# Two heads in one DMA transpose, the hash in row and column tiles, and TensorE in an order fixed by hand

## The chip, the cores and the metric

The kernel runs on one core of a Trainium2 chip. The metric is device time in microseconds (us), from the program's start to its end on that core. A run has a state, "fast" or "slow" (slow: more than 1.5% above the fastest run of the same kernel). The clock is the share of its full speed that TensorE was granted, 0.50 being half. In the profiler's lines PE is TensorE, PEld its weight loads, DVE VectorE, ACT ScalarE, POOL GpSimd and SP SyncE; a q behind the name is the engine's queue, which here issues transfers.

## The reference, cut to what matters

There are 4 batches, 8 heads, 768 tokens per head and 64 features. Each query and each key gets six bits from the signs of a projection, and a query attends only to keys whose six bits equal its own. The attention's output goes through a gated feed-forward part with 3072 tokens, width 512 and hidden width 1536.

```python
q_bits = (np.einsum('bhsd,dk->bhsk', q, proj) > 0).astype(np.int64)
k_bits = (np.einsum('bhsd,dk->bhsk', k, proj) > 0).astype(np.int64)
...
scores = np.where(q_bucket[..., None] == k_bucket[:, :, None, :],
                  scale * np.matmul(q, k.transpose(0, 1, 3, 2)), -1e9)
attn = softmax(scores)                      # cut: exp, sum, divide
x = (attn @ v) as (3072, 512)
out = x + sigmoid(x @ w_res) * ((gelu(x @ w_gate) * (x @ w_val)) @ w_out)
```

## The kernel before

The mask is part of the scores' matmul. Behind the 64 features of a token stand 7 more rows: six hash bits of +-0.5, and a constant. The query features are scaled down by C and the exponential scales up again, so a pair of tokens that differs in a bit gets a very negative score. The scores therefore contract over 71 rows.

Work goes by pairs of heads (16 pairs, two pairs to a group). `prep` makes a group's operands: cast, hash, bits, transpose. It is a Python generator, advanced one piece per step of the attention.

```python
nat = [const.tile([P, HT, P], BF16) ...]         # HT = 12 blocks: 2 heads x 6
def prep(ps, first=False):
    hs = mm_ps.tile([P, HT, 32], FP32, tag="mm", name="hs")   # one PSUM bank
    for i, x in enumerate(jobs):                 # jobs: q and k of each pair
        cast(x, ...)                             # nat[:, :, 0:64] = bf16(raw)
    for h in range(2):
        ... # VectorE: tt = 32x32 block transposes of raw
        for dh in range(2):
            for j, tt in enumerate(t32):
                nc.tensor.matmul(hs[32 * j:32 * j + 32, h * T:(h + 1) * T, :],
                                 projw[:, dh, :], tt[:, :, dh, :], ...,
                                 tile_position=(0, 32 * j))    # column tiles only
        yield
    nc.vector.transpose(ht[:n], hs[:n])
    for j, x in enumerate(jobs):
        for a in range(4):                       # bits into nat[:, :, 64:70]
            nc.vector.tensor_scalar(nat_of(x)[32 * a:32 * a + 32, :, D:D + NBITS], ...)
        nc.sync.dma_start_transpose(out=ag, in_=nat_of(x))     # 12 blocks of 128x128
        aug[x] = ag
        yield
```

One step of the attention is a double bank of scores, one exponential over 128x1024, and the value matmuls of the step before. Each batch has 36 steps. The feed-forward part of batch b-1 is done during the attention of batch b: `gate_val` in one block, then `project` in pieces between the steps. The projection's two accumulators (`rps`, `fps`) and the hash share one pool of two PSUM banks, `mm_ps`.

```python
sc_ps = tile_pool("sc_ps", bufs=2, space=PSUM)   # scores: two double banks
av_ps = tile_pool("av_ps", bufs=2, space=PSUM)   # attention accumulators
mm_ps = tile_pool("mm_ps", bufs=2, space=PSUM)   # projection and hash
def scores(p, c):
    sp = sc_ps.tile([P, 1024], FP32, tag="sp", name="sp")
    ... # ks[0:71, block] x qs[0:71, up to 512 columns]
    nc.scalar.activation(e, sp, AF.Exp, scale=float(ALPHA))
    flush()                                      # the values of the step before
```

The softmax here doesn't subtract the row's maximum and nothing guards it: scores larger than these inputs give would overflow.

Of the kernel before, what the change touches and what calls it, by code (L numbers as in the profile page):

```python
# [9 lines left out]
FP32 = mybir.dt.float32  # L10
BF16 = mybir.dt.bfloat16
AF = mybir.ActivationFunctionType
ALU = mybir.AluOpType
# [4 lines left out]
def kernel(  # L18
# [11 lines left out]
):  # L30
    nc = tc.nc
    B, H, S, D = q.shape
    NBITS = proj.shape[1]
# [9 lines left out]
    NROW = NBITS + 1  # L43
    KA = D + NROW
    assert D == 64 and S == 768 and 4 * NBITS <= 32 and HP == KM

# [9 lines left out]


    projw = const.tile([P, 2, 32], FP32, name="projw")
    nc.vector.memset(projw, 0.0)
    for a in range(4):  # L60
        nc.scalar.dma_start(projw[32 * a:32 * a + 32, :, NBITS * a:NBITS * (a + 1)],
                            proj.rearrange("(h r) n -> r h n", r=32))
# [5 lines left out]

    NN = 4
    nat = []  # L70
    for i in range(NN):
        nat.append(const.tile([P, HT, P], BF16, name=f"nat{i}"))
        eng = nc.vector if i < 2 else nc.gpsimd
        eng.memset(nat[i][:, :, D:P], 0.0)
        eng.memset(nat[i][:, :, D + NBITS:KA], 1.0 if i % 2 == 0 else -NBITS / 4.0)

# [25 lines left out]
    ld_pool = ctx.enter_context(tc.tile_pool(name="ld", bufs=3))  # L102
    ldv_pool = ctx.enter_context(tc.tile_pool(name="ldv", bufs=2))
    aug_pool = ctx.enter_context(tc.tile_pool(name="aug", bufs=4))
    t32_pool = ctx.enter_context(tc.tile_pool(name="t32", bufs=5))
# [4 lines left out]
    av_ps = ctx.enter_context(tc.tile_pool(name="av_ps", bufs=2, space=PSUM))  # L110
    mm_ps = ctx.enter_context(tc.tile_pool(name="mm_ps", bufs=2, space=PSUM))

    raw, rawv, aug, vaug = {}, {}, {}, {}
# [14 lines left out]

    def nat_of(x):
        return nat[(2 * x[0] + x[1]) % NN]  # L130

    def cast(x, eng):
        scale = (1.0 / C) if x[1] == 0 else 1.0
        dst = nat_of(x)[:, :, 0:D]
        if eng is nc.scalar:
            nc.scalar.activation(dst, raw[x], AF.Copy, scale=scale)
        elif x[1] == 0:
            eng.tensor_scalar(dst, raw[x], scale, 1.0, op0=ALU.mult, op1=ALU.mult)  # L138
        else:
            eng.tensor_copy(dst, raw[x])  # L140

# [14 lines left out]
    def prep(ps, first=False):  # L156

        jobs = [(p, side) for p in ps for side in range(2)]
        n = 32 * len(jobs)
        hs = mm_ps.tile([P, HT, 32], FP32, tag="mm", name="hs")  # L160
        for i, x in enumerate(jobs):
            cast(x, nc.scalar if first and i == 0 else nc.gpsimd)
        yield
        for h in range(2):
            t32 = []
            for x in jobs:
                tt = t32_pool.tile([P, T, 2, 32], FP32, tag="t32", name="t32")
                nc.vector.transpose(tt.rearrange("p c h n -> p (c h n)"),  # L168
                                    raw[x][:, h * T:(h + 1) * T].rearrange("p c d -> p (c d)"))
                t32.append(tt)  # L170
                if len(t32) % 2 == 0:
                    yield
            for dh in range(2):
                for j, tt in enumerate(t32):
                    nc.tensor.matmul(hs[32 * j:32 * j + 32, h * T:(h + 1) * T, :],  # L175
                                     projw[:, dh, :], tt[:, :, dh, :],
                                     start=(dh == 0), stop=(dh == 1),
                                     tile_position=(0, 32 * j))
            yield
        ht = sm_pool.tile([P, HT, 32], FP32, tag="ht", name="ht")  # L180
        nc.vector.transpose(ht[:n].rearrange("p c n -> p (c n)"),
                            hs[:n].rearrange("p c n -> p (c n)"))
        for j, x in enumerate(jobs):
            del raw[x]
            for a in range(4):
                nc.vector.tensor_scalar(  # L186
                    nat_of(x)[32 * a:32 * a + 32, :, D:D + NBITS],
                    ht[32 * j:32 * j + 32, :, NBITS * a:NBITS * (a + 1)], 0.0, 0.5,
                    op0=ALU.is_gt, op1=ALU.subtract)
            ag = aug_pool.tile([P, HT, P], BF16, tag=f"aug{x[1]}", name=f"aug{x[1]}")  # L190
            nc.sync.dma_start_transpose(out=ag, in_=nat_of(x).rearrange("p c n -> p (c n)"))
            aug[x] = ag
            yield
        for p in ps:
            values_of(p)
            yield


    banks = []
    for hi in range(2):  # L200
        for i in range(T // 2):
            banks += [(hi, [(2 * i, 0, 4)]), (hi, [(2 * i + 1, 0, 4)]),
                      (hi, [(2 * i, 4, 2), (2 * i + 1, 4, 2)])]
    NCH = len(banks) // 2
    av = {}
# [15 lines left out]
    def values(p, c, e):  # L221
        va, vsum = vaug[p]
        for i in range(2):
            hi, parts = banks[2 * c + i]
            if (p, hi) not in av:
                o = av_ps.tile([P, T, D + 1], FP32, tag="av", name="av")
# [4 lines left out]
                    start=True, stop=False, skip_group_check=True)  # L231
            off = i * 512
            for (jt, qt0, nq) in parts:
                for qt in range(qt0, qt0 + nq):
# [3 lines left out]
                    off += P  # L238
            if (2 * c + i + 1) % NCH == 0:
                finish(p, hi)  # L240
# [7 lines left out]
    def scores(p, c):  # L248
        qs, ks = aug[p, 0], aug[p, 1]
        sp = sc_ps.tile([P, 1024], FP32, tag="sp", name="sp")  # L250
        for i in range(2):
            hi, parts = banks[2 * c + i]
            off = i * 512
            for (jt, qt0, nq) in parts:
                nc.tensor.matmul(sp[:, off:off + nq * P], ks[0:KA, hi * T + jt, :],  # L255
                                 qs[0:KA, hi * T + qt0:hi * T + qt0 + nq, :],
                                 start=True, stop=True)
                off += nq * P
# [28 lines left out]
    def project(b):  # L287

        hh = hidden.pop(b)
        for t in range(T):  # L290
# [4 lines left out]
            th = g_pool.tile([P, DMODEL], FP32, tag="th", name="th")  # L295
            nc.scalar.activation(th, rps, AF.Tanh, scale=0.5)  # L296
            yield
            fps = mm_ps.tile([P, DMODEL], FP32, tag="mm", name="fps")
            for m in range(KF):
                nc.tensor.matmul(fps, hh[:, m, bass.ts(t, P)], wo[:, m, :],  # L300
                                 start=(m == 0), stop=(m == KF - 1))
                if m % 3 == 2 and m < KF - 1:
# [5 lines left out]
                                           op0=ALU.mult, op1=ALU.add)  # L308
            nc.sync.dma_start(out_t[b, t], o)
            yield  # L310

# [17 lines left out]
    HELD = 6  # L329
    mlp = []  # L330

    def mlp_piece():
        while mlp:
            g = mlp[0]
            try:
                next(g[0])
                g[1] += 1
                return
            except StopIteration:
                mlp.pop(0)  # L340

    done = object()
    for g in range(NG):
# [61 lines left out]
```

## Time and profile before

| Before | Value |
|---|---|
| median of 2 runs | 407.11 us (406.05 to 408.16) |
| profiled run | span 404.7 us, mean clock 0.92 |
| part one: start to the first feed-forward matmul | 98.2 us |
| the three stretches that hold a feed-forward block beside attention | 84.3, 85.9, 78.1 us (sum 248.4 before rounding) |
| tail: the last feed-forward block | 58.2 us |

I call the three stretches "batches" below. They run from one block's first feed-forward matmul to the next block's first. Here they are as windows; the columns are length, busy time and instructions of PE, PEld, DVE, ACT and POOL, then clock, DMA share (1.00 means that all 16 DMA engines are busy) and GB/s.

```profile
0.00:98.18 98.18, 73.72 (x572) 35.36 (x575) 44.83 (x124) 42.20 (x42) 47.22 (x88) 0.68 1.11 225
98.18:182.50 84.32, 81.59 (x715) 47.20 (x725) 34.60 (x68) 51.14 (x57) 17.70 (x32) 0.98 0.54 115
182.50:268.40 85.90, 82.13 (x735) 47.50 (x744) 41.01 (x91) 51.30 (x57) 16.59 (x30) 1.00 0.48 104
268.40:346.50 78.10, 76.85 (x652) 44.11 (x662) 29.20 (x59) 48.94 (x54) 0.00 (x0) 1.00 0.21 49
```

In the batches TensorE is idle for only 1 to 4 us of about 80, so I expected that whatever is added to TensorE's queue there is paid nearly in full. (A busy PE in the profile is not PE at its peak.) In part one it is idle for 24 us, and its mean clock is 0.68.

From the page's groups, the rows that the change touches. A row gives busy us and the mean ns of one instruction, then the idle time ahead of them and what ended most of it. The last row is a DMA's median time from issue to landing.

```profile
L175 PE MATMUL hs<-t,projw 128*32 128x192 f32 x256 | 27.3, 375 | 17.8 <-DVE t L168 11.7
L186 DVE TENSOR_SCALAR nat<-ht 32x72 bf16<-32x72 f32 x128 | 31.3, 244 | 2.3
...
aug<-nat SPq DMA_TRANSPOSE x32, 4.9
```

### The profile page before, as it was taken

To read this page: it belongs to the slowest core of one execution; us is meant where nothing else is said; L and a number is where in the kernel's file an instruction comes from. 1 tells how busy PE (TensorE), PEld (TensorE's weight loads), DVE (VectorE), ACT (ScalarE), POOL (GpSimd) and SP (SyncE) were. 2 spreads that over 40 slices of the span, in tenths; PEclk is the share of its full clock that TensorE was granted. 3 is DMA by queue.
4 is the path that set the end of the run, shared out by engine and by line. 5 is a ranking of instruction groups with operands and counts; after the bars stand their busy time and mean duration, and the time that the engine had idled before them with its cause. 6 is when DMAs were issued, how large, how long until landed. Compare 5 with 4: busy or idle time off the path is not lost. (4 is left out here: it accounts for less than half of the span.)

```text
span 404.7 us, 7265 instructions
## 1 busy us (share of the span) xinstructions
PE 366.9 (91%) x2944; PEld 202.2 (50%) x2990; DVE 170.7 (42%) x366; ACT 206.9 (51%) x225; POOL 81.5 (20%) x149
## 2 busy tenths in 40 slices
PE   6386969959999999998999999899999999999995
PEld 2133524425566555554665555556655555565542
DVE  3727123715433324734336537443336232333342
ACT  2036534636332877773335886863357788333210
POOL 7456245344300022241000342310000000000000
PEclk9759555865999999999999999999999999999999
DMA  7999999996910048776000973920008221100012
GB/s 220 223 270 245 159 239 285 201 238 142 238 55 2 28 84 188 137 186 202 2 0 2 185 205 85 185 47 2 0 2 158 76 68 47 45 2 0 16 65 78
DMA packets 86177, 46.61 MB, mean 115 GB/s; under 512 B 64640, under 2 KB 83072, under 8 KB 86144
## 3 DMA queue, kind: packets, MB, share of 16 engines
q1 hardware_dynamic: 79488, 40.91, 44.7%
q0 software_dynamic: 6336, 5.24, 8.7%
q8 instruction: 23, 0.38, 0.4%
q14 instruction: 10, 0.08, 0.1%
q10 hardware_dynamic: 320, 0.01, 0.0%
HBM read 29.37 MB, written 6.29 MB: 88 GB/s over the span
## 5 line engine op out<-in xcount | busy, mean ns | idle before, releaser
L260 ACT ACTIVATE e<-sp 128x1024 bf16<-128x1024 f32 x144 | 144.4, 1022 | 83.8 <-PE sp L255 82.4
L255 PE MATMUL sp<-aug,aug 71*128 71x256 bf16 (+1 forms) x384 | 98.2, 362 | 4.3 <-DMA aug<-nat 4.1
L282 ACT ACTIVATE gt<-sp 128x768 bf16<-128x768 f32 x48 | 38.9, 810 | 83.3 <-PE sp L276 83.3
L283 DVE TENSOR_TENSOR hh<-gt,sp 128x768 bf16<-128x768 bf16 x48 | 45.8, 953 | 81.1 <-PE sp L276 81.1
L235 PEld LDWEIGHTS <-e 128*128 128x128 bf16 x1152 | 54.3, 104 | 43.1 <-ACT e L260 24.0
L276 PE MATMUL sp<-x_sb,wg 128*128 128x512 bf16 (+1 forms) x382 | 72.0, 328 | 2.6 <-DMA x_sb<-x_tok 2.1
L300 PE MATMUL fps<-wo,hh 128*128 128x512 bf16 x265 | 71.4, 379 | 1.7 <-issue 0.5
L276 PE MATMUL sp<-x_sb,wv 128*128 128x512 bf16 (+1 forms) x371 | 70.0, 324 | 1.2 <-DVE hh L283 0.5
L235 PE MATMUL av<-va,e 128*128 128x65 bf16 x1152 | 66.1, 204 | 2.2 <-ACT e L260 1.1
L168 DVE STREAM_TRANSPOSE t<-ld 128x384 f32<-128x384 f32 x64 | 33.8, 557 | 43.8 <-DMA ld<-in_q_dram 21.3
L276 PEld LDWEIGHTS <-wg 128*128 128x128 bf16 x384 | 37.5, 98 | 28.1 <-issue 3.9
L255 PEld LDWEIGHTS <-aug 71*128 71x128 bf16 x384 | 34.8, 105 | 32.4 <-issue 6.5
L276 PEld LDWEIGHTS <-wv 128*128 128x128 bf16 x384 | 37.7, 98 | 25.8 <-issue 1.2
L175 PE MATMUL hs<-t,projw 128*32 128x192 f32 x256 | 27.3, 375 | 17.8 <-DVE t L168 11.7
L300 PEld LDWEIGHTS <-hh 128*128 128x128 bf16 x288 | 24.3, 97 | 24.0 <-issue 5.3
L305 DVE SCALAR_TENSOR_TENSOR o<-th,fps 128x512 f32<-128x512 f32 x24 | 16.4, 683 | 39.4 <-PE fps L300 29.6
L186 DVE TENSOR_SCALAR nat<-ht 32x72 bf16<-32x72 f32 x128 | 31.3, 244 | 2.3
L214 DVE RECIPROCAL rec<-av 128x6 f32<-128x6 f32 x32 | 6.0, 187 | 56.0 <-PE av L235 56.0
L138 POOL TENSOR_SCALAR nat<-ld 128x768 bf16<-128x768 f32 x15 | 12.4, 829 | 73.8 <-DMA aug<-nat 73.8
L296 ACT ACTIVATE th<-rps 128x512 f32<-128x512 f32 x24 | 14.3, 596 | 21.0 <-PE rps L293 17.7
L145 POOL CAST va<-ldv 128x768 bf16<-128x768 f32 x16 | 13.2, 822 | 57.2 <-PE av L235 52.5
L293 PE MATMUL rps<-wr,x_sb 128*128 128x512 bf16 x88 | 24.3, 382 | 0.1
(34 smaller groups left out, 152.9 us busy)
## 6 DMA issues: line engine op xcount, KB each, us to landing
ld<-in_q_dram SPq DMA_DIRECT2D x16, 384.0 KB, 4.7
ld<-in_k_dram SPq DMA_DIRECT2D x16, 384.0 KB, 4.6
ldv<-in_v_dram SPq DMA_DIRECT2D x16, 384.0 KB, 5.0
out_dram<-o SPq DMA_DIRECT2D x24, 256.0 KB, 2.1
wg<-in_moe_w_gate_dram POOLq DMA_DIRECT2D x4, 384.0 KB, 9.6
wv<-in_moe_w_val_dram POOLq DMA_DIRECT2D x4, 384.0 KB, 7.1
wo<-in_moe_w_out_dram POOLq DMA_DIRECT2D x3, 512.0 KB, 10.7
aug<-nat SPq DMA_TRANSPOSE x32, 4.9
```

The source lines that it names most:

```text
L168: nc.vector.transpose(tt.rearrange("p c h n -> p (c h n)"), raw[x][:, h * T:(h + 1) * T].rearrange("p c d -> p (c d)"))
L175: nc.tensor.matmul(hs[32 * j:32 * j + 32, h * T:(h + 1) * T, :], projw[:, dh, :], tt[:, :, dh, :], start=(dh == 0), stop=(dh == 1), tile_p ...
L186: nc.vector.tensor_scalar(nat_of(x)[32 * a:32 * a + 32, :, D:D + NBITS], ht[32 * j:32 * j + 32, :, NBITS * a:NBITS * (a + 1)], 0.0, 0.5, o ...
L235: nc.tensor.matmul(av[p, hi][:, qt, :], e[:, off:off + P], va[:, hi, jt, 0:D + 1], start=False, stop=(jt == T - 1), skip_group_check=True)
L255: nc.tensor.matmul(sp[:, off:off + nq * P], ks[0:KA, hi * T + jt, :], qs[0:KA, hi * T + qt0:hi * T + qt0 + nq, :], start=True, stop=True)
L260: nc.scalar.activation(e, sp, AF.Exp, scale=float(ALPHA))
L276: nc.tensor.matmul(sp[:, c0:c1], w[:, kk, bass.ts(m, P)], xs[:, kk, c0:c1], start=(kk == 0), stop=(kk == KM - 1))
L282: nc.scalar.activation(gt, sp[:, 0:S], AF.Gelu)
L283: nc.vector.tensor_mul(hh[:, m, :], gt, ps[1][:, 0:S])
L293: nc.tensor.matmul(rps, x_sb[b][:, kk, t, :], wr[:, kk, :], start=(kk == 0), stop=(kk == KM - 1))
L300: nc.tensor.matmul(fps, hh[:, m, bass.ts(t, P)], wo[:, m, :], start=(m == 0), stop=(m == KF - 1))
L305: nc.vector.scalar_tensor_tensor(o, th, 1.0, fps, op0=ALU.add, op1=ALU.mult)
```

## The change

The intent is to halve the feature transposes and start them earlier. The features of two heads (2 x 64) fill a whole 128-wide block, so a pair's q or k takes 6 blocks, not 12. The bits are no longer transposed with them. The hash delivers them already transposed, because it uses row tiles (32 features at a time, each with its own token block) beside column tiles. It writes four PSUM banks per half group (one head of each of the two pairs), in two visits of two banks; a visit is one such run of hash matmuls.

The first head's 64 features are then rows 0 to 63 of `aug`, and its seven bit rows are moved over rows 64 to 70 by a small DMA. The second head's features arrive in rows 64 to 127. VectorE copies them into `second`, and another small DMA puts bits into rows 0 to 6. (The first head's bits overwrite rows that this copy reads, so their transfer has to wait for the copy.) That head's scores contract over 128 rows, with zeros between.

TensorE's instructions are kept in the order in which the program writes them. Before, the scheduler chose the order of every engine; it still does for all others.

```diff
+    ctx.enter_context(tc.manual_schedule(engines={mybir.EngineType.PE}))
...
+    mlp, rows_open = [], []
+    def close_rows():            # finish the projection row that holds mm banks
+        while rows_open:
+            mlp_piece()
...
+    def features(x, eng):        # cast two heads side by side
+        n = nat_pool.tile([P, T, 2, D], BF16, ...)
...
+        nc.sync.dma_start_transpose(out=ag, in_=n)      # 6 blocks
+        aug[x] = ag
...
-            for dh in range(2):
-                for j, tt in enumerate(t32):
-                    nc.tensor.matmul(hs[32 * j:...], projw[:, dh, :], tt[:, :, dh, :], ...,
-                                     tile_position=(0, 32 * j))
+            for a0 in (0, 2):
+                close_rows()
+                hs = [mm_ps.tile([P, T, 32], FP32, tag="mm", name="hs") for _ in range(2)]
+                for dh in range(2):
+                    for j, tt in enumerate(t32):
+                        for i in range(2):
+                            a = a0 + i
+                            nc.tensor.matmul(hs[i][32 * j:32 * j + 32],
+                                             projw[32 * a:32 * a + 32, dh, :],
+                                             tt[32 * a:32 * a + 32, :, dh, :], ...,
+                                             tile_position=(32 * a, 32 * j))
+                for i in range(2):
+                    a = a0 + i
+                    nc.vector.tensor_scalar(bits[:n, h, :, 32 * a:32 * a + 32], hs[i][:n],
+                                            0.0, cst[:n], op0=ALU.is_gt, op1=ALU.add)
+                yield
+            for j, (p, side) in enumerate(jobs):
+                if h == 1:
+                    nc.sync.dma_start(second[p % NM][side][0:NROW],
+                                      bits[32 * j:32 * j + NROW, h])
+        for j, (p, side) in enumerate(jobs):
+            ag = aug[p, side]
+            nc.vector.tensor_copy(second[p % NM][side][D:P], ag[D:P])
+            nc.sync.dma_start(ag[D:D + NROW], bits[32 * j:32 * j + NROW, 0])
...
-        qs, ks = aug[p, 0], aug[p, 1]
+        ops = ((D + NROW, aug[p, 0], aug[p, 1]), (P, *second[p % NM]))
```

A step now holds both heads of a pair, three steps to two key blocks, so both heads end in the same step. What else is cut: the preparation of `second`, `cst` and `projw`, the loops over the scores' banks, and the bookkeeping of `rows_open` in `project`.

## The prediction

> **What bounds the kernel now.** I first read the page's 40 slices, then a table of windows, then the timeline around the gaps. The slices split the kernel in two.
>
> ```profile
> PE   6386969959999999998999999899999999999995
> PEclk9759555865999999999999999999999999999999
> DMA  7999999996910048776000973920008221100012
> ```
>
> In the first ten slices (10 us each) the DMA engines are full, TensorE (PE) has gaps and its clock is often halved; afterwards TensorE is full at full clock and DMA is half idle. The first matmul of the feed-forward part (L276) starts at 98.2 us, so I cut there; columns are busy PE, PEld, DVE, ACT, POOL, then clock, DMA share, GB/s.
>
> ```profile
> 0.00:21.70 21.70, 9.78 (x48) 4.00 (x48) 11.10 (x32) 2.12 (x2) 12.80 (x28) 0.85 1.02 221
> 21.70:98.20 76.50, 63.96 (x524) 31.38 (x527) 33.73 (x92) 40.09 (x40) 34.44 (x61) 0.63 1.14 226
> 98.20:348.00 249.80, 241.94 (x2100) 139.47 (x2138) 105.97 (x218) 151.37 (x166) 34.26 (x62) 0.99 0.42 91
> 348.00:404.70 56.70, 51.26 (x276) 27.36 (x280) 19.93 (x25) 13.30 (x18) 0.00 (x0) 1.00 0.09 33
> ```
>
> So part one (98.2 us) is bound by transfers and the half clock, part two (306.5 us) by TensorE, which idles only 7.9 us of 249.8 before the tail. The costliest gaps of part one:
>
> ```profile
> 21.74 1.89 PE L255 MATMUL sp<-aug,aug 71*128 71x512 bf16 x5 [4.06 <-DMA aug<-nat]
> ...
> 40.11 0.85 PE L175 MATMUL hs<-t,projw 128*32 128x192 f32 x2 [2.85 <-DVE t L168]
> ```
>
> The scores wait for the transposed features (aug); the hash waits for its VectorE transposes, which wait for loads. The issuing queue shows why the loads are late: two feature transposes hold it from 36.13 us on for 10.23 us. The hash itself:
>
> ```profile
> 0.00:98.20 98.20, 19.44 (x128) 6.13 (x128) 0.68 1.11 225
> 98.20:404.70 306.50, 7.87 (x128) 3.56 (x128) 1.00 0.36 80
> ```
>
> ```profile
> 155.86 0.86 PE L175 MATMUL hs<-t,projw 128*32 128x192 f32 x16
> 156.65 0.82 PE L300 MATMUL fps<-wo,hh 128*128 128x512 bf16 x2
> ```
>
> The same 128 records cost 19.4 us in part one, scattered in ones and twos, and 7.9 us in part two, where 16 run together in 0.79 us (155.86 to 156.65).
>
> [...] here four feature transposes alone run at 212 to 216 GB/s (308 to 314 us), so 393 KB take 1.83 us. [...] the clock stays at 0.50 all through 40 to 50 us, although TensorE is 99% busy in it. [...]
>
> **The change part by part.**
>
> Transposes. A pair's q and k go from 12 blocks of 128x128 each to 6, so each from 1.83 to 0.92 us. They also no longer contain the hash bits, so they can start at the cast. Fourteen are issued before 98.2 us: 14 x 0.91 = 13 us of DMA time off a part that holds about 110 us of DMA share (98.2 x 1.11). In the changed order the first feed-forward matmul needs only pairs 0 to 5, and by 98 us the old kernel had loaded nine pairs. My estimate of what must have moved: seven to eight pairs of loads at 3 x 1.56 us (what is left of 110 after transposes 29, x_sb 4 and weights 35, over 27 loads) = 33 to 37, twelve transposes 11 to 12, x_sb 4, weights 25 to 35: 73 to 88 us of share, at 1.13 per us 65 to 78 us. Added: four transfers of 7 rows x 1.5 KB per pair, tiny in bytes, but each waits behind the loads (median 4.7 us now) and the scores wait for them.
>
> Start. The scores start at 21.7 us because cast, hash, bits and transpose are in series. After, transpose and hash run side by side, but the bits need a transfer and the hash of pair 1 stands ahead of the first scores in the fixed order (its inputs are there at about 17 us now). I give 19 us.
>
> From there to the first feed-forward matmul lie 40 steps; ScalarE needs 1.02 us each for the exponential (L260: 144.4 us over 144), 42 us with the hash in the slack if warm: 61 us at best. With transfers as the bound, I take 76 us instead of 98.2: **gain 22 us**, of which about 13 are the transposes, the rest order.
>
> Hash on TensorE. Four row tiles replace one block-diagonal: 1024 records instead of 256. A visit is now 32 records in 8 tiles, and a group of two pairs makes four visits instead of two. Each tile still streams four records, so if rows overlap as columns do, a visit takes the 0.79 us that 16 records in four tiles take now; if issue bounds it at the 28 ns between weight loads (14 begin within 0.36 us at 32.9 us) it takes 32 x 28 ns = 0.9 us[...]. Five groups lie in part two: 20 x 0.79 to 1.05 = 16 to 21 us against 7.9 (four groups now): **+8 to +13, say +11 us**, all on the bound engine.
>
> PSUM turns. A visit takes both `mm` banks, which the projection also uses, and the open projection row is finished just before. VectorE must first read that row out: in the tail this turn shows directly.
>
> ```profile
> 385.19 1.03 PE L293 MATMUL rps<-wr,x_sb 128*128 128x512 bf16 x4
> 385.44 0.69 DVE L305 SCALAR_TENSOR_TENSOR o<-th,fps 128x512 f32<-128x512 f32 x1 [2.17 <-PE fps L300]
> ...
> 386.19 1.02 PE L300 MATMUL fps<-wo,hh 128*128 128x512 bf16 x4
> ```
>
> From the row's last matmul issued (385.19) to the next matmul in its bank (386.19) is 1.0 us. Walking the program, the row is closed immediately ahead of a visit at slots 6, 10, 11 and 23 of each batch's 36: 4 x 1.0 us. After each of the four visits of the first half, the next projection matmul waits for VectorE to read a hash bank: 0.25 + 0.3 us = 0.6 us, four times. That is 6.4 us per batch, 18 us for three (the last has no slot 23): **+18 us**[...].
>
> Accumulators. Both heads of a pair now end in the same step, so the next pair's first accumulation waits for two rounds of L214 and L215 (0.19 + 0.55 us each): about 0.3 us beyond the work between, over 11 pairs: **+3 us**. And since closing rows uses the projection up early, about 16 instead of 7 steps per batch have only attention and are bound by the exponential (1.03 us against TensorE's 0.73): **+5 us** over three batches after hash visits fill some.
>
> VectorE. Away go 128 bit writes (31.3 us) and 9 transposes (5.1 us); in come 72 writes of 128x192 from PSUM at about 0.3 us (22 us) and 32 copies of 64x768[...]. VectorE is 42% busy; no gain by itself.
>
> Sum: 407.1 - 22 + 11 + 18 + 3 + 5 = 422 us.
>
> **The rivals.** *A, part one wins:* [...] ScalarE is the bound: 61 to 65 us, gain 35. For it: clock 0.50 over most of 40 to 72 and 84 to 98 us costs about half of that. If the PSUM turns are also hidden (half of +18), the total is about 407 - 35 + 11 + 9 + 3 + 5 = 400, with a hash at the low end 397. Against it: DMA is full throughout. *B, row tiles don't overlap:* eight tiles take two turns, 1.58 us a visit, 32 us instead of 16 to 21, giving about 435. For it: no record before shows row tiles.[...] *C, small transfers take the place of the transposes:* in part one the bits land 5 us late at each group, TensorE stops[...]; part one ends at 88 us, total about 434. *D, the order written by hand is simply the better one:* the stalls of part two are absorbed by queued work, and only hash is lost: 407 - 22 + 11 = 396.
>
> **Range and chances.** My step sum says 422, but the slot walk can be wrong and errors there mostly favour the change: the sum counts every turn as fully exposed. I give the sum two thirds and A and D together one third (about 395): 0.67 x 422 + 0.33 x 395 = 413 us. B and C are the upper end, A with D the lower: 388 to 433. Faster needs under 399, which in my sum takes a part one of 53 us, below the ScalarE limit, so only A or D give it: 0.26. Within 2% is 399 to 415: 0.31. Slower: 0.43.
>
> **What would show it.** Right: the first L276-type matmul well before 98 us (60 to 85) with fewer slices at half clock; feature transposes landing in about half the time; hash records x1024 with visits of 0.8 to 1.05 us; in part two, TensorE idle 20 us or more ahead of hash and `rps` matmuls, with VectorE's projection output and bit writes as the releasers; part two at 335 to 350 us instead of 306.5. Wrong: part two below 320 us (turns hidden, or row tiles very cheap), part one still near 95 us (transposes were not what delayed it), waits of scores for the bits' transfers of several us (rival C), or visits of 1.6 us (rival B).

The sum: 407.1 - 22 + 11 + 18 + 3 + 5 = 422 us. The hash's +11: the upper figure of 1.05 us a visit was 0.9 us plus 0.15 us without a source. With 0.9 the term would be +8 to +10 (20 x 0.9 = 18 against 7.9) and not +8 to +13, so the +11 stands as my estimate.

Column tiles overlap: 16 records in four of them took 0.79 us (155.86 to 156.65), and two records on their own 0.44 us at the same clock of 1.00 (31.26 to 31.70). Of the clock the trace shows that it was 1.00 from 37 to 39 us, in the gap of 2.85 us that ended at 40.11, and 0.50 from 40 to 50 us. That the fixed order would keep it full (rival A), or that a stop would halve it (rival C), was my assumption. The 0.3 us for a bit write is an estimate: L215 took 0.55 us for twice the width. 0.37 to 0.42 us were measured afterwards (changed kernel, L221).

## The result, and the profile after

The changed kernel takes 460.25 us (459.84 and 460.67) against 407.11. The ratio is 1.1306, with a 95% interval from 1.1172 to 1.1439. Ratios here are the mean time of one kernel's fast runs over the mean of the other's fast runs of the same rounds, so not quite the ratio of the medians that I quote. The prediction had the direction, but 460 lies 27 us above the top of its range.

| us, from the profiles | before | after | change | the prediction's sum |
|---|---|---|---|---|
| first scores, at | 21.7 | 40.1 | +18.4 | -2.7 (at 19) |
| part one | 98.2 | 99.9 | +1.8 | -22 |
| three batches | 84.3 + 85.9 + 78.1 | 101.9 + 105.5 + 94.1 | +53.1 | +37 |
| tail | 58.2 | 57.5 | -0.7 | 0 |

The slices of the page, each now 11.5 us long:

```profile
PE   4636848879988797789988797789988897799995
PEclk9555986999999999999999899989999999999999
DMA  8999997760003653870005643430000113200011
```

Beside the slices of before, TensorE's row has a regular pattern of 7s and 8s where it had 9s. These are the batches. The clock is better in part one, but part one doesn't end sooner. The windows show how much (columns as before):

```profile
0.00:99.93 99.93, 64.02 (x826) 33.83 (x835) 40.01 (x98) 41.74 (x43) 52.91 (x97) 0.78 1.00 207
99.93:201.80 101.87, 89.51 (x928) 50.41 (x940) 41.71 (x80) 51.35 (x57) 18.61 (x32) 1.00 0.41 88
```

TensorE's busy time in part one fell from 73.7 to 64.0 us, for more of it runs at full clock (mean 0.78 against 0.68), yet 36 us of idle time stand in 99.9. In the first batch it is idle for 12.4 us where it was idle for 2.7, and it is busy for 7.9 us longer. The transfers got what was promised. The share of the hardware queue, from the page's third part, was 44.7% of 404.7 us and is 33.2% of 458.9, so 28.5 us of all 16 engines' time went away; 32 transposes at 0.91 us less each are 29.

**The first 40 us.** This is the timeline around the first scores (start, duration, engine and so on; what ended the idle time before it is in brackets).

```profile
22.57 3.18 SPq L171 DMA_TRANSPOSE aug<-nat  x2
...
25.79 1.82 PE L214 MATMUL hs<-t,projw 32*32 32x192 f32 x16 [0.95 <-DVE bits L221]
...
33.45 0.36 DVE L231 COPY second<-aug 64x768 bf16<-64x768 bf16 x1 [6.91 <-DMA aug<-nat]
...
37.54 0.36 DVE L231 COPY second<-aug 64x768 bf16<-64x768 bf16 x1 [3.73 <-DMA aug<-nat]
...
37.93 0.73 DVE L221 TENSOR_SCALAR bits<-hs,cst 64x192 bf16<-64x192 f32 x2
...
38.39 1.82 PE L214 MATMUL hs<-t,projw 32*32 32x192 f32 x16 [10.78 <-DVE bits L221]
...
40.14 0.61 PE L293 MATMUL sp<-aug,aug 71*128 71x512 bf16 x1
```

Read it from the bottom. The first scores stand behind a hash visit in TensorE's fixed order. The visit waited 10.78 us for VectorE to read out the bank of the visit before (the `bits` at 37.93 us). VectorE had no work to do in that time. It stood in front of two copies (`second`), each of which waits for one of the two DMA transposes in the first line: by the semaphores in the trace, those issued at 22.57 and 24.47 us. They were not issued late. They landed at 33.43 and 37.51 us, 10.9 and 13.0 us after their issue, while the DMA share was 1.24 (22.57 to 37.51 us). In the compiled order of VectorE's instructions, these copies belong to pair 2, and the bit writes behind them to pair 1:

```
TensorCopy      second2_0_92 <- aug0_369   (pair 2)
TensorCopy      second2_1_94 <- aug1_373   (pair 2)
tensor_scalar   bits <- hs, cst   x2       (pair 1, 64 partitions)
StreamTranspose t32_436 <- ld1_352
tensor_scalar   bits <- hs, cst   x2       (pair 1, 64 partitions)
```

So two waits for operands that nobody needs yet (6.91 and 3.73 us) held up the bit writes that TensorE needed now (10.78 us).

**The rest of part one.** Two rows of the sums of waits from 0 to 99.93 us (total, times, longest):

```profile
DVE second L231 <- DMA aug<-nat: 31.0, 12, 8.5
...
PE hs L214 <- DVE bits L221: 20.3, 7, 10.8
```

The second is TensorE's own largest wait, and VectorE stood for 31.0 us in front of copies. One further hole of TensorE comes from the other new transfer, the bits':

```profile
58.25 8.37 SPq L171 DMA_TRANSPOSE aug<-nat  x2
...
66.71 3.00 SPq L226 DMA_DIRECT2D second<-bits  x4
...
69.98 0.61 PE L293 MATMUL sp<-second,second 128*128 128x512 bf16 x1 [5.84 <-DMA second<-bits]
```

VectorE had written these bits by 58.93 us. SyncE, which has two transposes ahead of these transfers in its order, was issuing them from 58.25 to 66.62 us, and the first two bit transfers landed 3.0 and 2.4 us after their issue. Here they are late because they were issued late.

**The batches.** First the hash itself, where the clock is full (this visit is near the end of part one):

```profile
85.46 0.88 PE L214 MATMUL hs<-t,projw 32*32 32x192 f32 x32
86.27 0.39 PE L293 MATMUL sp<-aug,aug 71*128 71x256 bf16 x2
```

From start to the next matmul it is 0.81 us for 32 records in eight tiles (four columns, two rows). Before, 16 records in four tiles took 0.79 us. So row tiles do overlap here (each writes a bank of its own). In the batches, a visit that finds a projection row open has a bank turn on both sides:

```profile
137.27 2.75 PE L338 MATMUL fps<-wo,hh 128*128 128x512 bf16 x12
139.95 0.51 PE L214 MATMUL hs<-t,projw 32*32 32x192 f32 x2
140.88 0.88 PE L214 MATMUL hs<-t,projw 32*32 32x192 f32 x30 [0.42 <-DVE o L343]
142.68 1.02 PE L330 MATMUL rps<-wr,x_sb 128*128 128x512 bf16 x3 [0.93 <-DVE bits L221]
```

The row is closed in one go (12 `fps` matmuls), the visit gets two records out and goes on 0.93 us after its start (139.95 to 140.88), when VectorE has read `fps`, and the next `rps` waits 0.93 us for the bit writes. Summed over the batches, by what TensorE waited for:

```profile
PE av L274 <- ACT e L297: 11.0, 26, 0.9
...
PE rps L330 <- DVE bits L221: 8.5, 12, 0.9
...
PE hs L214 <- DVE o L343: 5.3, 11, 1.2
```

The last two rows are the turn, 13.8 us. The first is the exponential that nothing covers once the projection's work is used up. The end of part one, where there is no projection yet, shows the same: the values that TensorE waits for start at 89.83, 91.86 and 93.89 us, two exponentials of 1.02 us apart.

### The profile page after: what moved, and what is told of

It is laid out like the page before. It is cut to its first block, busy times and chain, and to the rows that moved or that the text cites. A ratio compares the mean times of both kernels' runs of the same rounds, so it can differ in the third digit from the quotient of the medians.

```text
span 458.9 us, 8897 instructions
## 1 busy us (share of the span) xinstructions
PE 382.3 (83%) x3700; PEld 210.0 (46%) x3758; DVE 172.2 (38%) x333; ACT 206.2 (45%) x225; POOL 85.3 (19%) x154
## 3 DMA queue, kind: packets, MB, share of 16 engines
q1 hardware_dynamic: 55808, 35.30, 33.2%
## 5 line engine op out<-in xcount | busy, mean ns | idle before, releaser
L274 PEld LDWEIGHTS <-e 128*128 128x128 bf16 x1152 | 51.5, 100 | 57.5 <-ACT e L297 47.2
L313 PE MATMUL sp<-x_sb,wg 128*128 128x256 bf16 (+1 forms) x381 | 70.4, 325 | 1.1 <-DMA x_sb<-x_tok 1.0
L313 PE MATMUL sp<-x_sb,wv 128*128 128x256 bf16 (+1 forms) x372 | 69.6, 324 | 0.6
L214 PE MATMUL hs<-t,projw 32*32 32x192 f32 x1024 | 45.2, 349 | 25.7 <-DVE bits L221 20.3
L293 PE MATMUL sp<-aug,aug 71*128 71x512 bf16 x192 | 57.5, 340 | 2.0 <-DVE hh L320 2.0
L293 PE MATMUL sp<-second,second 128*128 128x256 bf16 (+1 forms) x172 | 49.3, 332 | 8.5 <-DMA second<-bits 8.5
L333 ACT ACTIVATE th<-rps 128x512 f32<-128x512 f32 x24 | 14.3, 597 | 70.8 <-PE rps L330 70.7
L214 PEld LDWEIGHTS hs<-t,projw 32*32 32x32 f32 x1024 | 21.8, 109 | 44.0 <-DVE bits L221 24.7
L201 DVE STREAM_TRANSPOSE t<-ld 128x384 f32<-128x384 f32 x64 | 33.6, 558 | 17.5 <-PE hs L214 13.4
L221 DVE TENSOR_SCALAR bits<-hs,cst 128x192 bf16<-128x192 f32 (+1 forms) x72 | 26.0, 401 | 22.7 <-PE hs L214 22.6
L231 DVE COPY second<-aug 64x768 bf16<-64x768 bf16 x32 | 14.2, 449 | 54.0 <-DMA aug<-nat 53.9
L169 POOL CAST nat<-ld 128x768 bf16<-128x768 f32 x16 | 13.9, 869 | 94.9 <-DMA ld<-in_k_dram 90.3
```

The lines of the kernel that those rows point to most:

```text
L201: nc.vector.transpose(tt.rearrange("p c h n -> p (c h n)"), raw[x][:, h * T:(h + 1) * T].rearrange("p c d -> p (c d)"))
L214: nc.tensor.matmul(hs[i][32 * j:32 * j + 32], projw[32 * a:32 * a + 32, dh, :], tt[32 * a:32 * a + 32, :, dh, :], start=(dh == 0), stop=(d ...
L221: nc.vector.tensor_scalar(bits[:n, h, :, 32 * a:32 * a + 32], hs[i][:n], 0.0, cst[:n], op0=ALU.is_gt, op1=ALU.add)
L274: nc.tensor.matmul(av[p, hi][:, qt, :], e[:, off:off + P], va[:, hi, jt, 0:D + 1], start=False, stop=(jt == T - 1), skip_group_check=True)
L293: nc.tensor.matmul(sp[:, off:off + nq * P], ks[0:n, jt, :], qs[0:n, qt0:qt0 + nq, :], start=True, stop=True)
L313: nc.tensor.matmul(sp[:, c0:c1], w[:, kk, bass.ts(m, P)], xs[:, kk, c0:c1], start=(kk == 0), stop=(kk == KM - 1))
```

## The experiments

Fifteen kernels ran, in four calls; each call has its own runs of the kernel before (medians 409.12, 410.18, 411.39 and 409.00 us). All edits are to the changed kernel unless the label begins with b, which is the kernel before. Theory one: part one's gain is eaten by two new waits (the copies in VectorE's queue, and the late bits' transfers), and the batches lose to bank turns. Rival one: the fixed order is the whole cause. Rival two: the eight-tile hash is the cost. Rival three: halving the transposes saves no time to begin with.

### Is it the fixed order? (e1, b1, e2)

**e1** drops the fixed order from the changed kernel.

```diff
-    ctx.enter_context(tc.manual_schedule(engines={mybir.EngineType.PE}))
```

> The changed kernel with only the fixed TensorE order taken out, so the scheduler orders TensorE as it did before. Theory O (the fixed order is the main cost: TensorE stands still behind waits that other work could fill): most of the 53 us come back, 410 to 425 us, and the first scores start before 25 us instead of 40.1. Theory W (the work itself is: hash in 1024 records, two PSUM banks per visit, bits by transfer): at most 15 us come back, 445 to 460 us. Mine is in between: start repaired (about 15 us) and the turns partly filled (about 10), 430 to 440 us.

It took 450.68 us in its fast run and 459.22 in its profiled run, which is slow, so its parts are only a hint. In that profile the batches fell to 276.7 us from 301.5, but part one rose to 120.2 us. Its windows from 40 us on:

```profile
40.00:60.00 20.00, 20.00 (x192) 8.83 (x190) 8.33 (x18) 9.22 (x9) 9.07 (x14) 0.50 1.14 211
60.00:80.00 20.00, 20.00 (x178) 8.92 (x167) 7.02 (x18) 10.24 (x10) 5.50 (x11) 0.50 0.79 165
80.00:100.00 20.00, 20.00 (x163) 8.40 (x160) 4.01 (x10) 8.19 (x8) 4.14 (x9) 0.50 0.31 84
```

TensorE counts as busy throughout, and the clock is granted at half for all of it. The order is not the whole cause: without it the fast run is still 41.6 us above the median of the kernel before.

**b1** puts the fixed order on the kernel before, and nothing else.

```diff
+    ctx.enter_context(tc.manual_schedule(engines={mybir.EngineType.PE}))
```

> The kernel before with only TensorE's order fixed to the program's. Theory O (the fixed order is the main cost): 425 us or more. Theory W (what is hashed and how is the cost, the order is harmless or good): 395 to 412 us, since the hash's single records of part one, 19.4 us, come together.

412.15 us, ratio 1.0068 (0.9938 to 1.0198): the same. Inside, it is a trade: part one 92.0 us (6.2 less), the batches 259.0 (10.6 more). If one adds the time from each matmul's start to TensorE's next start, by line, the scores take 56.6 us of the batches instead of 49.8. Nothing is added to the scores' work; TensorE waits behind them more often. Its waits for the exponential over the batches, before and then in b1:

```profile
PE av L235 <- ACT e L260: 0.8, 3, 0.3
```

```profile
PE av L236 <- ACT e L261: 5.5, 15, 0.7
```

Its waits for `x_sb` (the transposed attention output) also rose, from 1.8 to 3.7 us, and one hash visit of 16 records moved across my cut. These are 7 to 8 of the 10.6 us; I didn't pin down the rest.

**e2** fixes VectorE's order as well, so that pair 1's bit writes come before pair 2's copies.

```diff
-    ctx.enter_context(tc.manual_schedule(engines={mybir.EngineType.PE}))
+    ctx.enter_context(tc.manual_schedule(engines={mybir.EngineType.PE, mybir.EngineType.DVE}))
```

> The changed kernel with VectorE's order fixed to the program's too. Theory H (in the start VectorE stands behind copies of pairs 2 and 3, which the scheduler placed ahead of the bits of pair 1, while TensorE's fixed order puts pair 1's hash ahead of the first scores): the 10.8 us gap goes, first scores at 22 to 28 us instead of 40.1, whole 442 to 450 us. Rival (the transposes themselves land late whatever VectorE's order is, as the DMA engines are full): first scores still after 35 us, whole 455 to 465 us.

461.70 us, ratio 1.1278 (1.1127 to 1.1428): nothing gained. TensorE's 10.8 us wait is gone and the first scores start at 29.9 us, but the waits turn up as scores waiting for bits, and part one ends at 104.6. From its sum of waits over part one, and the largest of them:

```profile
PE sp L293 <- DMA aug<-bits: 21.2, 4, 12.3
```

### What do the bank turns cost? (e3)

**e3** writes the hash into one double bank of the scores' pool in place of two `mm` banks. No projection row has to be closed.

```diff
-                close_rows()
-                hs = [mm_ps.tile([P, T, 32], FP32, tag="mm", name="hs") for _ in range(2)]
+                hb = sc_ps.tile([P, 1024], FP32, tag="sp", name="hs")
+                hs = [hb[:, 512 * i:512 * i + 32 * T].rearrange("p (t n) -> p t n", n=32)
+                      for i in range(2)]
```

> The changed kernel with the hash written to one of the two double banks of the scores instead of both banks of the projection, and without closing the projection row first. Theory P (turns of the projection's banks and the early using up of the projection make 30 us or more of the loss): waits of hash for the projection's output (5.3 us) and of rps for the bits (8.5 us) go, steps with attention alone fall from 16 to about 7 per batch, whole 430 to 445 us. Rival (the turn only moves to the banks of the scores, so the exponential waits instead): 452 to 462 us.

428.22 us, ratio 1.0460 (1.0396 to 1.0524), so 32 us better than the change. The batches are 271.2 us, 30.3 less. The visit now stands without a wait on either side:

```profile
132.19 0.88 PE L215 MATMUL hs<-t,projw 32*32 32x192 f32 x32
133.01 1.04 PE L331 MATMUL rps<-wr,x_sb 128*128 128x512 bf16 x4
```

By elapsed time (from each hash matmul's start to TensorE's next start), the hash takes 17.1 us of e3's batches, against 37.1 in the changed kernel and 7.9 in the kernel before. The first scores start at 24.4 us instead of 40.1, but part one remains at 97.7 us. All labels with e below build on e3, since its batches are clean. One thing to keep in mind there: the hash now sits in the scores' banks, so scores also wait when VectorE is late with reading the hash out.

### Which of the two new waits holds part one? (e4, e5, e8, e9, e10, e11, e12)

**e4** is e3 with VectorE's order fixed (as in e2), **e5** is e4 with the bits' transfers issued by GpSimd.

```diff
-                    nc.sync.dma_start(second[p % NM][side][0:NROW],
+                    nc.gpsimd.dma_start(second[p % NM][side][0:NROW],
...
-            nc.sync.dma_start(ag[D:D + NROW], bits[32 * j:32 * j + NROW, 0])
+            nc.gpsimd.dma_start(ag[D:D + NROW], bits[32 * j:32 * j + NROW, 0])
```

> Hash in the banks of the scores (428.2 us as it was) and VectorE's order fixed as well. Theory H (what is left of the loss in part one is VectorE standing behind hoisted copies that wait for transposes, 8.0 us at one place and 3.1 at another): 412 to 420 us. Rival Q (the wait moves on to the transfers of the bits, which queue behind loads and transposes, as in the run with VectorE's order fixed alone, where scores waited 22.9 us for them): 425 to 435 us.

> The same, with the transfers of the bits issued from GpSimd's queue instead of SyncE's, behind the transposes. If Q holds because of the order in the issuing queue: 10 us or more below the run without, 405 to 415 us, waits for bits under 5 us. If Q holds because the 16 DMA engines are full: no change within 4 us. If GpSimd's own order holds them up (casts behind waits): slower, 435 us or more.

e4: 434.67 us (1.0613), e5: 443.24 us (1.0823). Both are slower than e3, with part one at 106 us in both. Scores wait 30.3 us for the first head's bits in e4 and 34.3 in e5. In e5 the bits' transfers land a median of 2.6 to 2.7 us after issue over the whole kernel, but that mixes two regimes: in part one, where these waits are, the medians are 5.8 and 6.3 us, and after it 1.9. The longest wait of scores, 14.9 us (to 70.50 us), has both parts: the two transfers that it needs were issued 8.5 and 9.0 us into it (64.07 and 64.57), and then took 5.7 and 5.9 us to land.

**e8** moves the copies to GpSimd:

```diff
-            nc.vector.tensor_copy(second[p % NM][side][D:P], ag[D:P])
+            nc.gpsimd.tensor_copy(second[p % NM][side][D:P], ag[D:P])
```

> Hash in the banks of the scores (428.2 us), and the 32 copies of the second head's features on GpSimd instead of VectorE. Theory V (part one stays long because VectorE, in order, stands behind copies that wait for transposes, and the bits, the loads' transposes and the accumulators' read-out stand behind it): part one 97.7 to 85 or less, whole 412 to 418 us. Rival B (the transfers of the bits gate the scores anyway): part one within 4 us, whole 425 to 432 us.

421.34 us, ratio 1.0239 (1.0093 to 1.0384): the best correct version, and still not faster than the kernel before. Part one is 96.2 us. VectorE no longer stands before transposes, and now a single wait for the bits' transfer takes nearly the same amount:

```profile
54.86 2.97 SPq L227 DMA_DIRECT2D second<-bits  x4
...
66.54 0.59 PE L294 MATMUL sp<-second,second 128*128 128x512 bf16 x1 [15.66 <-DMA second<-bits]
```

The four transfers are issued by 57.83 us, and the scores go on at 66.54, 8.7 us later, for transfers of 10.5 KB. The scores need the first two; by the semaphore records in the trace these were issued at 54.86 and 55.67 and landed 11.3 and 10.7 us later. So most of the 15.66 us here is the landing, and not the issue as at 66.71 us in the changed kernel. e3 has a hole of the same kind.

To separate the two, the next three leave parts out. Their results are wrong. (The comparison with the reference passes e9 all the same: its second head has no features left, but these barely move the output at the tolerance used. It isn't a valid version.) **e9** leaves the copies out and keeps the bits' transfers. **e10** leaves the transfers out and keeps the copies on VectorE. **e11** leaves out both. (In e9 and e11 `second` is zeroed whole, as nothing fills its upper rows.)

```diff
-            nc.vector.tensor_copy(second[p % NM][side][D:P], ag[D:P])          # e9, e11
...
-                    nc.sync.dma_start(second[p % NM][side][0:NROW],            # e10, e11
-                                      bits[32 * j:32 * j + NROW, h])
...
-            nc.sync.dma_start(ag[D:D + NROW], bits[32 * j:32 * j + NROW, 0])   # e10, e11
```

> Wrong result on purpose: hash in the banks of the scores, the copies left out (the second head's features stay zero). Theory V: part one 85 us or less, whole 408 to 416 us. Rival B: within 4 us of 428.

> Wrong result on purpose: hash in the banks of the scores, the transfers of the bits left out, the copies kept. Theory V: little, 422 to 428 us, as VectorE still stands behind the copies. Rival B: part one 85 us or less, whole 410 to 416 us.

> Wrong result on purpose: neither copies nor transfers of bits. This leaves of part one only loads, transposes of half the size, hash and attention. If the halved transposes are worth what the prediction said, part one is 76 us or less here, and the two removed together explain the missing gain: whole 402 to 408 us. If part one is still above 88 us, the loads and weights bind it and the gain was never there.

| e3 and ... | part one | whole kernel |
|---|---|---|
| e3: copies and transfers | 97.7 us | 428.22 us |
| e9: transfers only | 102.1 us | 426.34 us, 1.0360 |
| e10: copies only | 110.4 us | 449.48 us, 1.0923 |
| e11: neither | 84.8 us | 416.78 us, 1.0128 |

With e8 (transfers only as far as VectorE is concerned: 96.2 us), either one suffices to hold part one at 96 us or more, and only when both are gone does it end at 85. In e9 the scores' waits are for the transfers (the two rows are the second head's bits and the first head's):

```profile
PE sp L293 <- DMA second<-bits: 18.6, 2, 14.0
...
PE sp L293 <- DMA aug<-bits: 7.7, 1, 7.7
```

In e10 hash and scores wait for VectorE to read the hash out of its banks (its bit writes do that), and VectorE stands before the copies. TensorE's rows first, then VectorE's largest row of this kind over the whole kernel:

```profile
PE hs L215 <- DVE bits L222: 28.0, 11, 9.2
PE sp L289 <- DVE bits L222: 21.8, 6, 11.5
```

```profile
DVE second L228 <- DMA aug<-nat: 53.7, 19, 13.4
```

e10 is slower than e3, which has these copies too, so the two waits don't simply add up. I take it that without the transfers, transposes and copies fall at other times, but that is not shown. e11 still has one hole of its own of 9.0 us, values that wait for VectorE's attention read-out; VectorE had stood for 10.3 us, until 77.96, in front of a hash transpose whose load had not landed. Note also that even e11, with nothing left of the two waits, is not faster than the kernel before (1.0128, interval 0.9944 to 1.0312): its part one is 13.4 us shorter and its batches are 22.4 us longer (270.7 us).

**e12** is e8 with the bits' transfers of the first groups (up to pair 6) issued by ScalarE, whose queue has no other transfers then (15 to 70 us). Its question was whether the bits land sooner from a queue other than SyncE's, which issues the large transfers.

```diff
+        bq = nc.scalar if ps[0] < 6 else nc.sync
...
-            nc.sync.dma_start(ag[D:D + NROW], bits[32 * j:32 * j + NROW, 0])
+            bq.dma_start(ag[D:D + NROW], bits[32 * j:32 * j + NROW, 0])     # and second's
```

> Hash in the banks of the scores, copies on GpSimd (421.3 us), and for the first six pairs the bits' transfers are issued from ScalarE's queue[...]. Theory R (the bits land late[...]: issued at 54.9 to 57.8 us, the scores go on at 66.5): waits of scores for bits fall from 22 us to under 8, part one from 96.2 to 82 to 88 us, whole 408 to 414 us. Rival (all 16 engines are full,[...] or ScalarE's exponentials now stand behind the issues): part one above 93 us, whole 418 us or more.

425.01 us over four runs, ratio 1.0349 (1.0261 to 1.0437). TensorE's own wait for bits is almost gone (1.3 us for transfers over the whole kernel). But now ScalarE issues them in front of an exponential, and TensorE waits for that (5.89 us, to 56.85):

```profile
50.93 4.74 ACTq L228 DMA_DIRECT2D second<-bits  x4
55.77 1.94 ACT L299 ACTIVATE e<-sp 128x1024 bf16<-128x1024 f32 x2 [6.34 <-DMA second<-bits]
```

Part one is 98.3 us. The profiler names the transfer as what ended the 6.34 us, but the exponential doesn't read `second`. What stands there is the issuing, as the trace's single records show: four issues of 0.72 to 0.73 us, and ahead of the first two of them 1.45 and 1.77 us in which ScalarE waits. The transfers themselves land 5.8 to 6.1 us after issue, against 9.7 to 11.3 us for the same four in e8. So in this pair of profiles the transfers landed sooner on ScalarE's queue, and the issuing took the gain away.

### Is the transposes' saving real? (e6, b2, b3)

**e6** issues each feature transpose of e3 twice (the second into a scratch tile), which makes the transfers as expensive as before.

```diff
+        twice = nat_pool.tile([P, T, P], BF16, tag="twice", name="twice")
+        nc.sync.dma_start_transpose(out=twice, in_=n.rearrange("p t h d -> p (t h d)"))
```

> Hash in the banks of the scores, with each feature transpose issued twice (the second into a tile nobody reads), so the transposes move as many bytes as before the change. The prediction gave the halving 13 us of part one. If that is so: part one (97.7 us to the first feed-forward matmul) grows by 10 to 16 us, whole 438 to 445 us. Rival (part one waits for order and latency, not for bytes): under 4 us, 427 to 432 us.

469.74 us, ratio 1.1469: 41.5 us above e3, 21 of them in part one and 16 in the first batch. The transfers added are an estimated 29 us (32 of 0.91). Values wait once for 15.2 us on VectorE's read-out, and hash for 13.0 us on bit writes. The loss exceeds what was added; I take it that VectorE, with copies in its queue, passes a delay of the transposes on to all that stands behind them, but no run separates that. e6 is no measure of the transposes in the old kernel; it measures how strongly the new one hangs on them.

**b2** is the measure. It is the kernel before with only the first head's six blocks transposed, used for both heads (wrong), and **b3** adds the fixed order.

```diff
-            nc.sync.dma_start_transpose(out=ag, in_=nat_of(x).rearrange("p c n -> p (c n)"))
+            nc.sync.dma_start_transpose(out=ag[:, 0:T], in_=nat_of(x)[:, 0:T].rearrange("p c n -> p (c n)"))
...
-                nc.tensor.matmul(sp[:, off:off + nq * P], ks[0:KA, hi * T + jt, :],
-                                 qs[0:KA, hi * T + qt0:hi * T + qt0 + nq, :],
+                nc.tensor.matmul(sp[:, off:off + nq * P], ks[0:KA, jt, :],
+                                 qs[0:KA, qt0:qt0 + nq, :],
```

> Wrong result on purpose: the kernel before with feature transposes of half the size (only the first head of a pair, whose features both heads then use); nothing else. This is the saving of the change without its new steps. The prediction said 13 us for the halving: part one 98.2 to 83 to 88 us, whole 392 to 399 us. If part one was bound by loads and order instead: 402 to 408 us.

> Wrong result on purpose: the same with TensorE's order fixed too. If the fixed order adds its 3 us as it did on the full kernel before: 395 to 403 us; if the halved transposes remove the waits that the fixed order exposed (15.6 us for aug): 385 to 393 us.

b2: 399.14 us, ratio 0.9721 (0.9635 to 0.9806), part one 93.5. b3: 397.88 us, ratio 0.9699 (0.9591 to 0.9806), part one 83.9. The saving is real, about 10 us of the whole, and with the fixed order part one loses 14.3 us. As a window, part one of b3:

```profile
0.00:83.93 83.93, 60.30 (x562) 30.81 (x562) 35.29 (x103) 42.92 (x43) 46.69 (x87) 0.77 1.09 230
```

The transfers are as dense as in the kernel before (1.09 against 1.11), and there is only less to transfer. In the changed kernel the share is 1.00, and its last two slices of part one show 7 and 6 tenths: the DMA engines have room there while TensorE waits.

### Is it the hash's stream? (e7)

**e7** makes only the first of two visits and writes all bits from it: 512 records instead of 1024 (wrong).

```diff
-            for a0 in (0, 2):
+            for a0 in (0,):
...
-                for i in range(2):
-                    a = a0 + i
-                    nc.vector.tensor_scalar(bits[...], hs[i][:n], ...)
+                for a in range(4):
+                    nc.vector.tensor_scalar(bits[...], hs[a % 2][:n], ...)
```

> Wrong result on purpose: hash in the banks of the scores, with the second visit of each pair of visits left out (512 records instead of 1024; VectorE writes all bits from the first). It gives the price of hashing by four row tiles on TensorE: with 0.8 to 1.0 us per visit and 18 visits gone, 14 to 18 us if exposed, 410 to 414 us. If the visits hide in the time that TensorE waits for the exponential: under 6 us, 422 us or more.

428.83 us, ratio 1.0471: the same as e3. The batches are 269.3 us against 271.2. The run hides the stream's price, because the edit also makes one double bank of the scores wait for four bit writes instead of two. Inside the batches the two cancel: the hash's elapsed time falls from 17.1 to 8.1 us, and the scores' waits for bit writes rise from 0.3 to 8.8 us. Rival two, that the stream is the main cost, falls by e3 rather than by e7: with all 1024 records left, e3 regains 32 of the 53 us.

## Why the prediction was right or wrong

The direction was right, and so was the view that the bank turns cost most in the batches. The sum said 422 us, and 460 was measured. Of the missing 39 us (from the profiles, where the change is +54.2 and not +15), 24 are in part one and 16 in the batches.

**The step that failed: "I take 76 us instead of 98.2: gain 22 us."** It came out as +1.8. Its two halves were about 13 us for the transposes and the rest for order. The order alone gave 6.2 (b1), and half the transposes gave 8.1 more on top of it (b3 against b1). So 14 us were to be had, 8 fewer than I took. The remaining 16 (99.9 against b3's 83.9) were eaten by waits that the change itself makes, and the runs show two. First, a copy on VectorE that waits for a DMA transpose held everything behind it, bit writes and read-outs that TensorE needs (VectorE stood for 31.0 us in front of copies in part one of the changed kernel, and TensorE for 10.78 us behind two of them). I priced these copies by their duration ("no gain by itself"; they took 0.45 us each) and not by what they wait for. Second, the bits' transfers come late and scores stand for them. They are late in two ways, by the issue behind transposes in SyncE's order (7.8 us at 58.93) and by the landing (11 us in e8). Each of the two waits holds part one at 96 us or more (e8 and e9, e10); without both it is 84.8 (e11), 12.9 less than in e3. I saw the second ("the scores wait for them") and gave it no term in the sum; it stood only as rival C.

**"I give 19 us" for the first scores.** 40.1 were measured. I assumed that pair 1's hash would be done by then because its inputs are there. I checked the data's arrival, but not the order on the engine that empties the banks, which the scheduler still chose. In the changed kernel itself 21 of the 24 us lie here: from the first scores on, part one takes 59.8 us, against the 57 of my sum. But the late start is not a cause of its own, since e2 and e3 start at 29.9 and 24.4 us and end part one at 104.6 and 97.7. My budget of part one also counted 29 us of transposes, where the fourteen that I name make 26 (14 x 1.83); that shifts the estimate by some 3 us and is not the step that failed.

**PSUM turns (+18) and projection used up early (+5).** e3 takes both away and regains 30.3 us in the batches. The number of turns was as I walked it (11 waits ahead of a visit and 12 behind one), and so was about their size: 0.93 us against 1.0 ahead of the visit shown, and behind it 0.7 on average (8.5 over 12) and 0.93 at most, against 0.6. The mechanism was right, the size of the two terms together 7 us low.

**The hash's stream (+11).** Visits take 0.81 us and up, inside the predicted 0.79 to 1.05. By elapsed time e3's hash costs 9.2 us more than before in the batches, including its small waits. That is close, and e7 agrees as far as it goes: half the records took 9.0 us less of elapsed time, which came back as another wait. (0.15 us of the 1.05 was given no source.) Rival B (1.58 us a visit) is refuted.

**Accumulators (+3).** TensorE's wait for the attention read-out at the first accumulation is 1.9 us over the batches.

**A term that was missing: the fixed order in the batches.** I gave it no cost at all, and in rival D even took it for the better order. b1 shows 10.6 us lost in the batches. If the three add, which no run tests, the account of the batches is 30.3 + 9.2 + 10.6 = 50 of the measured 53 us; the last 3 I didn't separate.

**The rivals and the range.** Rival A expected a full clock and a part one of 61 to 65 us. The clock did rise, from 0.68 to 0.78, but TensorE's idle time rose too, from 24 to 36 us. Mixing A and D into the sum moved it from 422 to 413, further from the truth. My claim that errors "mostly favour the change" was the reverse of what happened: my sum left out the waits that I didn't name, and here those added. Two of my own signs of being wrong came true: part one near or above 95 us, and scores that wait several us for the bits' transfers (rival C, which expected 88 us of part one and 434 in all).

**What stays open.** What a shorter hash stream would be worth to the whole kernel; why e10 is slower than e3; why the small transfers take 10 us and more at some places of part one and 2 us at others; and why the clock stays at half while TensorE is counted busy (0.50 from 40 to 50 us in the kernel before, with 9.89 of these 10 us busy, and 0.50 from 40 to 100 us in e1's slow run, with all of it busy). No correct version that I ran beats the kernel before. Half the transposes alone would (b2, 0.9721, with wrong results), if bits and features could be brought together without a wait that holds up the work behind it; I have found no such way.

## What to carry to other kernels

When a change replaces one long transfer by a short one plus a copy and small moves, price each new instruction by what it waits for and what stands behind it in its queue, not by its duration (here copies of 0.45 us each, and 31.0 us of waits in front of them in part one). When a small transfer is added, ask which queue issues it, what is issued ahead of it there, and how full the DMA engines are at that time: the same 10.5 KB took 1.9 us after e5's part one and about 6 in it (medians). Before giving a gain to an earlier transfer, list every wait that lies between it and the consumer, and take them all away in one run (as e11 does) to see the ceiling. When the order of one engine is fixed by hand, look at the orders of the engines that empty its buffers, for they are now part of its order.
